# Bias groups one to a step, a third bias buffer and larger zero transfers in a fused attention and mixture-of-experts kernel

## The chip, the cores and the metric

The kernel runs on one core of one Trainium2 chip. The metric is the device time of one execution in microseconds (us), lower is better; a time is the median of several executions. Engines are named as in the profile: PE is TensorE (matmuls; PEld its weight loads), DVE is VectorE, ACT is ScalarE, POOL is GpSimd, SP is the sync engine, which here issues nearly all DMA transfers from one queue, in program order. TensorE's granted clock is given as a share of 2.4 GHz.

## What is computed

Attention with a learned relative bias over B = 2, H = 8 heads, S = 576 positions and D = 64, then a routed layer of eight experts (top 1, capacity 288), then a dense layer with a cosine gate. The change lies in the attention and in the setting up of the routed layer's buffers.

```python
def _attn_ref(q, k, v, w1, b1, w2):
    scores = scale * np.matmul(q, k.transpose(0, 1, 3, 2))
    ...
    x = (psi_rel / psi_i)[..., None]            # of the two positions alone
    h = np.maximum(x @ w1 + b1, 0.0)            # 32 hidden values per pair
    bias = h @ w2                               # one value per head
    scores = scores + bias.transpose(2, 0, 1)[None, :, :, :]
    scores = scores - np.max(scores, axis=-1, keepdims=True)
    attn = np.exp(scores)
    attn = attn / (np.sum(attn, axis=-1, keepdims=True) + 1e-09)
    return np.matmul(attn, v)
def _moe_ref(x, w_gate, w1, w2, capacity):      # tokens go to disp[e, pos] of their expert,
    ...                                         # rows beyond its count stay empty
def _moe2_ref(x, w_in, w_out):
    h = x @ w_in
    return (h * np.cos(h)) @ w_out
```

The bias depends on the positions alone, so it is made once for the five blocks of rows and used for both batches.

## The kernel before

Query rows are cut into five blocks ib, four of 128 rows and one of 64 (ib 4). They are worked on in the order 0, 1, 4, 2, 3, each for batch 0 and then 1; only block 4 takes both batches at once and is called the joint block. That makes nine blocks of four head pairs, 36 steps n; steps 0 to 7 are block 0, 8 to 15 block 1, 16 to 19 the joint block, 20 to 27 block 2, 28 to 35 block 3. The queues' order is that of the program: one loop (L775) writes for each n the scores of step n + 1 (`emit_qk`, L343, two heads, with the sum of scores and bias on VectorE at L363, which also gives the row's extreme), the transposes of step n (L386, evicted by ScalarE at L393), the exponential of step n + 1 (L372), and the product with v of step n - 1 (L402, L405).

Between them the bias is made, in 36 groups: 8 for each block of 128 rows, 4 for the joint block. A group has four h tiles of 128x576 (`bias_h`, L288 on VectorE or L286 on ScalarE), two halves of four matmuls (`bias_half`, L311) into one PSUM buffer psb that ScalarE evicts (L312) into one of three ev buffers, and a transfer (`bias_out`, L297 or L301) that spreads the rows over the bias buffer of its block. Groups 0 to 7 come before the loop in a form of their own (`bias_whole`, L318, and L326), groups 8 and 9 just ahead of it. The table `RUNS` (L53) says which groups a step makes: groups 10 to 19 in steps 0 to 9, none in 10 to 13, two in each of 14 to 17, one in each of 18 to 25. It has to be so because there are two bias buffers, bias_a and keep, used in turn by the blocks in their order, and a buffer takes a new block only when the old one is read.

Split precision: q and k are kept as a high part (a cast, `load_q` L272, `load_k` L241) and a low part, the subtraction at L273 and L245. GpSimd does the low part of k and, after the first block, that of q; VectorE does the first ones. `load_step` (L731) brings k and v along in the early steps; raw k passes through three buffers.

The routed layer needs rows of disp that no token fills to hold zeros and an invalid index, and the output to be zero where no row arrives. From step 5 to 13 `fill_rows` (L742) sends them on SP's queue: each disp part of 144 rows as a transfer of 128 rows and one of 16, and for every other part 128 rows of zeros to the output. Routing work (`late`, run one piece a step) begins at step 14 (`ROUTE_FROM`); its products lp (L484) and its sums (L551) read a free quarter of a transposes' PSUM tile, and its scatters (L572) run on GpSimd after the fills.

Of the kernel before, what the change touches and what calls it, by code (L numbers as in the profile page):

```python
# [21 lines left out]
NP = H // 2  # L22
# [30 lines left out]
RUNS = {n: (g,) for g, n in [(10 + i, i) for i in range(10)] + [(28 + i, 18 + i) for i in range(8)]}  # L53
RUNS.update({14 + i: (20 + 2 * i, 21 + 2 * i) for i in range(4)})
# [53 lines left out]
def attention_moe_kernel(  # L108
# [100 lines left out]
    kr_p = rpool("kr_p", 1)  # L209
# [52 lines left out]
    def load_q(b, ib, lo_eng, on_act=False):  # L262
        raw = raw_t.pop(("q", b, ib))
# [9 lines left out]
        lo_eng.tensor_tensor(out=c, in0=raw, in1=a.bitcast(F32), op=ALU.subtract)  # L273
# [44 lines left out]
    def bias_whole(g):  # L318
        ev_t[g] = keep[:, g, :]
# [23 lines left out]
    def emit_qk(n, u):  # L343
# [8 lines left out]
        for half in range(2):  # L352
# [42 lines left out]
    def emit_pv(n):  # L395
# [1064 lines left out]
```

## Time and profile before

| | us |
|---|---|
| median of 3 executions | 450.65 |
| lowest, highest | 450.21, 454.18 |
| profiled execution, its own time | 454.37 |
| its span, first to last instruction | 452.6 |
| PE, DVE, ACT, POOL busy | 405.5, 333.0, 287.2, 89.1 |
| mean granted clock of TensorE | 0.972 |

The span is one execution as the hardware profiler saw it. Busy times are sums over stages with different limits, so the stretches of time are to be read one by one. "Idle before" with an arrow names what ended an engine's wait. The attention's steps take the first 230 us, the experts and the dense layer the rest.

### The profile page before, as it was taken

To read this page: it belongs to the slowest core of one execution; us is meant where nothing else is said; L and a number is where in the kernel's file an instruction comes from. 1 tells how busy PE (TensorE), PEld (TensorE's weight loads), DVE (VectorE), ACT (ScalarE), POOL (GpSimd) and SP (SyncE) were. 2 spreads that over 40 slices of the span, in tenths; PEclk is the share of its full clock that TensorE was granted. 3 is DMA by queue.
4 is the path that set the end of the run, shared out by engine and by line. 5 is a ranking of instruction groups with operands and counts; after the bars stand their busy time and mean duration, and the time that the engine had idled before them with its cause. 6 is when DMAs were issued, how large, how long until landed. Compare 5 with 4: busy or idle time off the path is not lost. (4 is left out here: it accounts for less than half of the span.)

```text
span 452.6 us, 9167 instructions
## 1 busy us (share of the span) xinstructions
PE 405.5 (90%) x3326; PEld 321.4 (71%) x3326; DVE 333.0 (74%) x809; ACT 287.2 (63%) x651; POOL 89.1 (20%) x129
## 2 busy tenths in 40 slices
PE   8958798998978999999988959988899999999992
PEld 6435565786434677697768949976588998999981
DVE  3789999768566578679864996978956787787750
ACT  5747767876355678887863735545666766666561
POOL 1005523200022122223062343000730000000004
PEclk9989999999799999999998999998999999999997
DMA  6696565788923323282449009999320222210003
GB/s 212 170 319 182 163 172 182 197 234 255 281 89 109 85 54 100 65 252 95 141 131 354 1 16 348 308 300 386 103 90 0 95 55 86 93 49 0 1 1 114
DMA packets 48495, 66.64 MB, mean 147 GB/s; under 512 B 7125, under 2 KB 30037, under 8 KB 48442
## 3 DMA queue, kind: packets, MB, share of 16 engines
q1 hardware_dynamic: 47273, 63.50, 46.8%
q0 software_dynamic: 1168, 2.48, 1.5%
q8 instruction: 28, 0.46, 0.4%
q14 instruction: 26, 0.20, 0.2%
HBM read 43.97 MB, written 11.54 MB: 123 GB/s over the span
## 5 line engine op out<-in xcount | busy, mean ns | idle before, releaser
L288 DVE TENSOR_SCALAR h<-tt,sml 128x576 f32<-128x576 f32 x124 | 72.0, 630 | 9.7 <-PE psb L311 9.7
L372 ACT ACTIVATE e<-e,mn 128x576 f32<-128x576 f32 x72 | 55.9, 776 | 16.0 <-DVE mn L363 16.0
L311 PE MATMUL psb<-h,sml 128*32 128x288 f32 x448 | 40.6, 431 | 10.5 <-ACT wo L312 10.2
L362 PE MATMUL pss<-k,qh 128*128 128x288 f32 x128 | 42.4, 347 | 3.7 <-DVE k L245 3.7
L405 PE MATMUL xb<-et,wi 128*64 128x128 f32 (+1 forms) x640 | 41.4, 272 | 0.0
L362 PEld LDWEIGHTS pss<-k,qh 128*128 128x128 f32 x128 | 24.4, 191 | 22.9 <-issue 18.8
L1277 PE MATMUL z<-yh,s1h 128*128 128x384 f32 (+1 forms) x128 | 39.7, 310 | 0.9 <-DVE yl L1230 0.9
L1277 PE MATMUL z<-yh,s1l 128*128 128x384 f32 (+1 forms) x128 | 39.5, 309 | 0.0
L1277 PE MATMUL z<-yl,s1h 128*128 128x384 f32 (+1 forms) x128 | 39.5, 309 | 0.0
L312 ACT ACTIVATE wo<-psb,sml 128x288 f32<-128x288 f32 x56 | 28.0, 500 | 16.9 <-PE psb L311 16.8
L363 DVE CUSTOM_DVE_ANT_0 e<-pss,keep 128x576 f32<-128x576 f32 x32 | 24.1, 755 | 19.8 <-PE pss L362 19.8
L363 DVE CUSTOM_DVE_ANT_0 e<-pss,bias 128x576 f32<-128x576 f32 x40 | 30.0, 750 | 9.2 <-PE pss L356 6.4
L362 PE MATMUL pss<-k,ql 128*128 128x288 f32 x128 | 36.3, 298 | 0.0
L405 PEld LDWEIGHTS xb<-et,wi 128*64 128x64 f32 x640 | 32.4, 139 | 4.5 <-issue 0.2
L1302 PE MATMUL oacc<-s2h,gh 128*128 128x512 f32 x80 | 31.2, 390 | 0.4 <-ACT gh L1327 0.4
L1302 PE MATMUL oacc<-s2h,gl 128*128 128x512 f32 x80 | 31.3, 391 | 0.0
L1302 PE MATMUL oacc<-s2l,gh 128*128 128x512 f32 x80 | 31.2, 390 | 0.0
L1317 DVE TENSOR_TENSOR tn<-tn,kn 128x640 f32<-128x640 f32 (+2 forms) x18 | 13.5, 752 | 21.6 <-ACT kn L1314 21.6
L970 PE MATMUL acc<-hl,s2h 128*128 128x288 f32 x64 | 20.9, 326 | 8.2 <-DVE hl L983 8.1
L273 POOL TENSOR_TENSOR ql<-qraw,qh 128x1024 fp32r<-128x1024 f32 x7 | 16.7, 2381 | 51.1 <-DVE qh L272 39.6
L1290 POOL DMA_INDIRECT out_dram<-o,id x5 | 4.9, 983 | 109.6 <-ACT o L1289 108.3
L311 PEld LDWEIGHTS psb<-h,sml 128*32 128x32 f32 x448 | 9.1, 110 | 23.1 <-ACT wo L312 16.6
(713 smaller groups left out, 1113.6 us busy)
## 6 DMA issues: line engine op xcount, KB each, us to landing
keep<-win SPq DMA_DIRECT2D x16, 512.0 KB
keep<-wout SPq DMA_DIRECT2D x16, 512.0 KB
w1r<-mw SPq DMA_DIRECT2D x12, 512.0 KB
w2r<-mw SPq DMA_DIRECT2D x12, 512.0 KB
disp<-wo SPq DMA_DIRECT2D x18, 258.0 KB
keep<-wo SPq DMA_DIRECT2D x16, 288.0 KB
qraw<-qd SPq DMA_DIRECT2D x8, 512.0 KB
wi<-kd SPq DMA_DIRECT2D x6, 576.0 KB
```

Source lines behind the costliest of these rows:

```text
L273: lo_eng.tensor_tensor(out=c, in0=raw, in1=a.bitcast(F32), op=ALU.subtract)
L288: V.tensor_scalar(out=h, in0=win_, scalar1=col, scalar2=0.0, op0=ALU.add, op1=ALU.max)
L311: T.matmul(out=ps[32 * j:32 * j + 32, :], lhsT=w2s, rhs=h_t[g, j][:, c0:c0 + 288], start=True, stop=True)
L312: A.activation(out=ev_t[g][:, c0:c0 + 288], in_=ps, func=AF.Copy, scale=rst[:, g:g + 1])
L362: T.matmul(out=ps[:, half, 0:288], lhsT=w[b, ib][:, h, :], rhs=kp[b, p][:, u, cols], start=(i == 0), stop=(i == 1))
L363: V.tensor_tensor_reduce(out=e_t[n][:, u].rearrange("p (a c) -> p a c", a=2), in0=ps[:, :, 0:288], in1=bias_t[ib][:, h].rearrange("p (a c) ...
L372: A.activation(out=e_t[n][:, u], in_=e_t[n][:, u], func=AF.Exp, scale=-1.0, bias=mn_t[n][:, u:u + 1], accum_out=z_t[b, ib][:, h:h + 1],)
L405: T.matmul(out=xo[64 * u:64 * u + 64], lhsT=v[:, 64 * (4 * u + j):64 * (4 * u + j) + 64], rhs=et[:, 5 * u + j, a:e], start=False, stop=(j ...
L970: T.matmul(out=acc[d], lhsT=a[g % 3][:, 128 * d:128 * d + 128], rhs=x[m % 2], start=(m == 0 and i == 0), stop=(m == 7 and i == 2),)
L1277: T.matmul(out=sums(f, i), lhsT=w[f % 3][:, k], rhs=x[:, k, o0 + a:o0 + e], start=(k == 0 and n == 0), stop=(k == 3 and n == 2),)
L1302: T.matmul(out=acc_[t], lhsT=x, rhs=b[f % 3], start=(f == 0 and n == 0), stop=(f == 15 and n == 2))
L1317: V.tensor_tensor(out=tn, in0=tn, in1=kn, op=ALU.subtract)
```

## The change

Bias: `RUNS` now gives one group to each of steps 0 to 26, groups 9 to 35. A third bias buffer takes the joint block; it is made of the part of the weight buffer wi through which raw k passed in the early steps. Block 0 uses keep, block 1 bias_a, block 2 keep, block 3 bias_a. A joint group is written to partitions 0 to 63 alone, and behind the last one transfer copies these to 64 to 127. In steps 6, 18 and 26 (`SOON`), whose group is the last of a block that the next step begins to read, the two halves stand at the front of the step. One group (8) is left ahead of the loop; the first step's sums come behind its halves.

q, k, v: the low part of q is VectorE's from now on, in two halves in the last two steps of the block before. The first k and q are brought in among the groups 0 to 7. Raw k has four buffers. The tiles of v are cut up to fit beside them, and two small buffers are added.

Fills: disp in ten transfers of 256 rows and one of 32 in steps 7 to 12; the output's nine in steps 15 to 23. The order in which columns of wi are filled later (`PIECE`) follows the new layout.

```diff
-RUNS = {n: (g,) for g, n in [(10 + i, i) for i in range(10)] + [(28 + i, 18 + i) for i in range(8)]}
-RUNS.update({14 + i: (20 + 2 * i, 21 + 2 * i) for i in range(4)})
+RUNS = {n: n + 9 for n in range(27)}
+SOON = 6, 18, 26
...
-    kraw = [wi[:, 2 * i:2 * i + 2, 1280:1280 + S] for i in range(2)]
+    KC = 1024 - S
+    kraw = [wi[:, i].rearrange("p (u s) -> p u s", u=2)[:, :, KC:1024] for i in range(4)]
...
-    bias_t = {ib: (bias_a, keep)[i % 2] for i, ib in enumerate(IBS)}
+    bias_t = {0: keep, 1: bias_a, 4: wi, 2: keep, 3: bias_a}
+    joint = wi.rearrange("p k (x s) -> p (k x) s", x=2)[:, :, KC:1024]
...
-        lo_eng.tensor_tensor(out=c, in0=raw, in1=a.bitcast(F32), op=ALU.subtract)
+    def load_q_lo(b, ib, hs=slice(0, H)):
+        if b != BOTH:
+            V.tensor_tensor(out=ql[b, ib][:, hs], in0=raw_t["q", b, ib][:, hs], in1=qh[b, ib][:, hs].bitcast(F32), op=ALU.subtract)
...
-            for c in range(B):
-                for rr in range(2):
-                    Y.dma_start(out=bt[64 * c + r + rr:64 * c + 64:8], in_=ev[64 * rr:64 * rr + 64])
+            for rr in range(2):
+                Y.dma_start(out=joint[r + rr:64:8], in_=ev[64 * rr:64 * rr + 64])
+            if r == 6:
+                Y.dma_start(out=joint[64:128], in_=joint[0:64])
...
+    among = {
+        1: (lambda: fetch_k(0, 2),),
+        3: (lambda: load_k(0, 0, on_act=True),),
+        4: (lambda: load_k_lo(0, 0, V),),
+        5: (lambda: load_q(*first_q, on_act=True),),
+        6: (lambda: load_q_lo(*first_q),),
+    }
     for g in range(8):
...
         bias_whole(g)
         bias_whole_out(g)
-    load_k(0, 0, on_act=True)
-    load_q(0, IBS[0], V, on_act=True)
-    warm(28)
-    load_k_lo(0, 0, V)
+        for f in among.get(g, ()):
+            f()
...
-    def fill_rows(k):
-        for j in range(k, k + 2):
-            Y.dma_start(out=disp[144 * j:144 * j + 128, :], in_=zr)
-            Y.dma_start(out=disp[144 * j + 128:144 * j + 144, :], in_=zr[0:16])
-            if j % 2 == 0:
-                Y.dma_start(out=out[64 * j:64 * j + 128, :], in_=zr[:, :DM])
+    LOADS = {-1: 2, 0: 3, 1: -1, 2: 4, 3: 5, 4: 6, 5: 7}
...
+    def fill_rows(a, n=256):
+        k = -(-n // 128)
+        Y.dma_start(out=disp[a:a + n, :].rearrange("(p k) d -> p k d", k=k), in_=zr[0:n // k, None, :].to_broadcast([n // k, k, RW]))
...
-                elif p == 2:
-                    load_q(*BLOCKS[j + 1], P)
+                if p == 2:
+                    load_q(*nb)
+                if p > 1:
+                    load_q_lo(*nb, slice(4 * p - 8, 4 * p - 4))
...
+            if soon:
+                bias_half(g, 0)
             emit_qk(n + 1, 0)
         if n < ns:
             emit_tr(n, 0)
+            if soon:
+                bias_half(g, 1)
...
-        if 5 <= n < 14:
-            fill_rows(2 * (n - 5))
+        if 7 <= n < 12:
+            for i in range(2):
+                fill_rows(256 * (2 * (n - 7) + i))
+        if n == 12:
+            fill_rows(2560, E1 * CAP - 2560)
+            fill_ids()
+        if 15 <= n < 24:
+            fill_out(n - 15)
```

`LOADS` says which k a step casts (the number is its place in the order of use); -1 stands for the second block's q.

The order shows three places. VectorE on the way from the last groups ahead of the loop to the first sums, before (k_346 and ql are the first k and q, k_382 the second k; L363 is the first sum):

```order
L288 TENSOR_SCALAR h<-tt,sml 128x576 x3
L329 TENSOR_SCALAR keep<-pss,sml 128x288 x2
L273 TENSOR_TENSOR ql<-qraw,qh 128x1024
L245 TENSOR_TENSOR k_346<-wi,k_346 64x1152
L685 TENSOR_SCALAR tt<-tt,sml 128x448
L241 CAST k_382<-wi 128x1152
L363 ISA e,mn<-pss,bias_130 128x576
```

And now (k_272 is the first k, k_401 the second, L397 the sum):

```order
L266 TENSOR_TENSOR k_272<-wi,k_272 64x1152
L312 TENSOR_SCALAR h<-tt,sml 128x576 x2
L354 TENSOR_SCALAR bias_126<-pss,sml 128x288
L312 TENSOR_SCALAR h<-tt,sml 128x576 x3
L354 TENSOR_SCALAR bias_126<-pss,sml 128x288
L297 TENSOR_TENSOR ql<-qraw,qh 128x1024
L354 TENSOR_SCALAR bias_126<-pss,sml 128x288
L718 TENSOR_SCALAR tt<-tt,sml 128x448
L262 CAST k_401<-wi 128x1152
L312 TENSOR_SCALAR h<-tt,sml 128x576
L266 TENSOR_TENSOR k_401<-wi,k_401 64x1152
L397 ISA e,mn<-pss,keep 128x576
```

The two subtractions moved in among the groups; the subtraction of the second k and one h tile now stand ahead of the first sum.

GpSimd from its first work for the steps to the first routing, before:

```order
L245 TENSOR_TENSOR k_477<-kraw,k_477 64x1152
L245 TENSOR_TENSOR k_542<-wi,k_542 64x1152
L273 TENSOR_TENSOR ql<-qraw,qh 128x1024
L245 TENSOR_TENSOR k_616<-wi,k_616 64x1152
L245 TENSOR_TENSOR k_686<-kraw,k_686 64x1152
L245 TENSOR_TENSOR k_760<-wi,k_760 64x1152
L273 TENSOR_TENSOR ql<-qraw,qh 128x1024
L496 TENSOR_SCALAR nm<-top 128x1
```

And now:

```order
L266 TENSOR_TENSOR k_430<-wi,k_430 64x1152
L266 TENSOR_TENSOR k_495<-wi,k_495 64x1152
L266 TENSOR_TENSOR k_638<-wi,k_638 64x1152
L266 TENSOR_TENSOR k_710<-wi,k_710 64x1152
L266 TENSOR_TENSOR k_779<-wi,k_779 64x1152
L529 TENSOR_SCALAR nm<-top 128x1
```

The q subtractions left GpSimd's queue; the five of k stayed.

TensorE in step 14, from the second transposes to the scores of step 16, before (pst__1517 holds transposes, k_829 is the k of step 15, xb the product with v):

```order
L386 MATMUL pst__1517<-ident,e 128x128 x3
L432 MATMUL pst__1517<-ident,wo 128x128
L311 MATMUL psb<-h,sml 32x288 x4
L362 MATMUL pss<-k_829,qh 128x288
L362 MATMUL pss<-k_829,ql 128x288
...
L311 MATMUL psb<-h,sml 32x288 x4
L386 MATMUL pst__1544<-ident,e 128x128 x3
L311 MATMUL psb<-h,sml 32x288 x4
L402 MATMUL xb<-et,wi 128x128
L405 MATMUL xb<-et,wi 64x128 x8
L311 MATMUL psb<-h,sml 32x288 x4
L356 MATMUL pss<-k_346,qh 64x288
```

And now (k_860 is the k of step 15, v_127 its v):

```order
L420 MATMUL pst__1508<-ident,e 128x128 x3
L465 MATMUL pst__1508<-ident,wo 128x128
L336 MATMUL psb<-h,sml 32x288 x4
L389 MATMUL pss<-k_860,qh 128x288
L389 MATMUL pss<-k_860,ql 128x288
...
L420 MATMUL pst__1532<-ident,e 128x128 x3
L435 MATMUL xb<-et,v_127 128x128
L438 MATMUL xb<-et,v_127 64x128 x8
L336 MATMUL psb<-h,sml 32x288 x4
L383 MATMUL pss<-k_272,qh 64x288
```

Of the four sets of bias matmuls two are left in this step.

## Rows read from the trace of the kernel before

**Rows 1.** Busy time by stretch: us, then each engine's busy time, granted clock, DMA.
```profile
core 0: us, PE busy (x) PEld busy (x) DVE busy (x) ACT busy (x) POOL busy (x), PEclk, DMA share, GB/s
20.00:37.30 17.30, 11.56 (x120) 7.54 (x116) 14.32 (x22) 9.11 (x16) 2.79 (x1) 0.90 0.90 278
37.30:73.20 35.90, 31.13 (x302) 20.96 (x296) 35.72 (x63) 24.77 (x63) 15.79 (x6) 1.00 0.56 159
...
110.40:149.60 39.20, 32.91 (x319) 16.60 (x317) 22.36 (x67) 20.07 (x51) 7.33 (x16) 0.91 0.58 171
149.60:193.40 43.80, 43.80 (x494) 31.38 (x494) 31.45 (x95) 33.42 (x86) 8.22 (x15) 1.00 0.29 79
...
113.50:119.20 5.70, 5.70 (x38) 2.99 (x38) 1.81 (x4) 2.14 (x5) 0.00 (x0) 0.50 0.84 256
```
**Rows 2.** Waits from 110.4 to 149.6 us: who for whom, us in total, times, longest.
```profile
PE psb L311 <- ACT wo L312: 6.3, 7, 2.4
```
**Rows 3.** Timeline of DVE around 111 us: start, us, engine, line, operation, tiles.
```profile
108.75 1.78 DVE L288 TENSOR_SCALAR h<-tt,sml 128x576 f32<-128x576 f32 x4
110.44 0.75 DVE L363 CUSTOM_DVE_ANT_0 e<-pss,keep 128x576 f32<-128x576 f32 x1
...
111.11 0.22 DVE L484 TENSOR_TENSOR lp<-pst__1499,rz 128x64 f32<-128x64 f32 x1
```
**Rows 4.** Timeline of ACT and of PE there; in brackets the idle time and its releaser.
```profile
111.43 0.49 ACT L393 ACTIVATE et<-pst__1499 128x384 f32<-128x384 f32 x1 [2.78 <-DVE lp L484]
...
113.50 1.19 PE L311 MATMUL psb<-h,sml 128*32 128x288 f32 x8 [2.35 <-ACT wo L312]
```
**Rows 5.** Groups of PE instructions from 149.6 to 193.4 us: busy us, mean ns.
```profile
L311 PE MATMUL psb<-h,sml 128*32 128x288 f32 x128 | 11.1, 418 | 0.0
```
**Rows 6.** Timeline of DVE at the entry of the loop.
```profile
24.10 1.22 DVE L273 TENSOR_TENSOR ql<-qraw,qh 128x1024 fp32r<-128x1024 f32 x1 [1.48 <-ACT qh L270]
25.35 1.35 DVE L245 TENSOR_TENSOR k<-wi,k 64x1152 fp32r<-64x1152 f32 x1
...
33.14 4.20 DVE L288 TENSOR_SCALAR h<-tt,sml 128x576 f32<-128x576 f32 x4
37.26 0.74 DVE L363 CUSTOM_DVE_ANT_0 e<-pss,bias 128x576 f32<-128x576 f32 x1
```
**Rows 7.** Timeline of ACT there: the casts of the first k and q.
```profile
21.97 1.15 ACT L239 ACTIVATE k<-wi 128x1152 fp32r<-128x1152 f32 x1
23.02 1.04 ACT L270 ACTIVATE qh<-qraw 128x1024 fp32r<-128x1024 f32 x1
```
**Rows 8.** Timeline of DVE: pairs of h tiles.
```profile
29.24 0.95 DVE L288 TENSOR_SCALAR h<-tt,sml 128x576 f32<-128x576 f32 x2
...
41.99 4.70 DVE L288 TENSOR_SCALAR h<-tt,sml 128x576 f32<-128x576 f32 x2
...
68.52 2.74 DVE L288 TENSOR_SCALAR h<-tt,sml 128x576 f32<-128x576 f32 x2
```
**Rows 9.** Timeline of POOL from 40 to 72 us.
```profile
40.77 3.04 POOL L245 TENSOR_TENSOR k<-wi,k 64x1152 fp32r<-64x1152 f32 x1 [4.61 <-DVE k L241]
43.89 2.47 POOL L273 TENSOR_TENSOR ql<-qraw,qh 128x1024 fp32r<-128x1024 f32 x1
...
68.16 2.35 POOL L273 TENSOR_TENSOR ql<-qraw,qh 128x1024 fp32r<-128x1024 f32 x1 [5.49 <-DVE qh L272]
```
**Rows 10.** Timeline of DVE at 205 and 211 us: a shift of the weight narrowing.
```profile
205.27 2.16 DVE L669 TENSOR_SCALAR wi<-wi 128x512 int32<-128x512 int32 x1
...
211.42 0.41 DVE L669 TENSOR_SCALAR wi<-wi 128x512 int32<-128x512 int32 x1
```
**Rows 11.** Timeline of SP (group 35's transfer) and of DVE (its first reader).
```profile
193.20 0.54 SPq L297 DMA_DIRECT2D bias<-wo  x1
...
197.08 0.76 DVE L363 CUSTOM_DVE_ANT_0 e<-pss,bias 128x576 f32<-128x576 f32 x1 [1.13 <-PE pss L362]
```

More of the change, by code (lines that the diff above doesn't have):

```diff
@@ L169, in attention_moe_kernel @@
     cut = lambda a, n: flat[:, a:a + n]
-    rows = [cut(RW * t, RW) for t in range(10)]
-    xs_buf = [cut(10 * RW + NP * 128 * i, NP * 128).rearrange("p (q t) -> p q t", q=NP) for i in range(2)]
-    base = 10 * RW + 2 * NP * 128
+    rows = [cut(RW * t, RW) for t in range(9)]
+    xs_buf = [cut(9 * RW + NP * 128 * i, NP * 128).rearrange("p (q t) -> p q t", q=NP) for i in range(2)]
+    base = 9 * RW + 2 * NP * 128
     lt_buf = cut(base, 128)
@@ L221, in attention_moe_kernel, with v_of, bias_of @@
     w1s, b1s, w2s, rst, pst = (sml[:, a:c] for a, c in SMALL_AT)
-    kp, vt = {}, {}
-    kraw.append(kr_p.tile([128, 2, S], F32, name="kraw"))
+    kp = {}
     bias_a = bias_p.tile([128, H, S], F32, name="bias0")
-    bias_t = {ib: (bias_a, keep)[i % 2] for i, ib in enumerate(IBS)}
+    bias_t = {0: keep, 1: bias_a, 4: wi, 2: keep, 3: bias_a}
+    joint = wi.rearrange("p k (x s) -> p (k x) s", x=2)[:, :, KC:1024]
+    v12 = kv_p.tile([128, 2, 640], F32, name="v12")
+    v_parts = {
+        (i // 4, i % 4): [(0, KC, beside[x]), (KC, 640, beside[y][:, z:z + 640 - KC])]
+        for i, (x, y, z) in enumerate([(0, 1, 0), (2, 1, 192), (3, 4, 0), (5, 4, 192), (6, 7, 0)])
+    }
+    for p in (1, 2):
+        v_parts[1, p] = [(0, 640, v12[:, p - 1])]
+    v_parts[1, 3] = [(0, 640, v13)]
+    def v_of(b, p, a, n):
+        for lo, hi, t in v_parts[b, p]:
+            if lo <= a and a + n <= hi:
+                return t[:, a - lo:a - lo + n]
+    def bias_of(ib, h):
+        if bias_t[ib] is wi:
+            return joint[:, h]
+        return bias_t[ib][:, h]
     raw_t = {}
     def fetch_k(b, p):
-        raw = kraw[(NP * b + p) % 3]
+        raw = kraw[(NP * b + p) % 4]
         Y.dma_start(out=raw, in_=kd[b, :, 2 * p:2 * p + 2, :])
@@ L247, in load_v @@
     def load_v(b, ps):
-        vt[b] = vt_buf[b]
         for p in ps:
-            Y.dma_start(out=vt[b][:, p], in_=vp[b, :, p])
+            for lo, hi, t in v_parts[b, p]:
+                Y.dma_start(out=t, in_=vp[b, :, p, lo:hi])
     qh, ql = {}, {}
@@ L318, in bias_whole @@
     def bias_whole(g):
-        ev_t[g] = keep[:, g, :]
+        ev_t[g] = bias_a[:, g, :]
         ps = ps_s.tile([128, 2, 512], F32, tag="s", name="pss")
@@ L400, in emit_pv @@
             xo = xb[:, 128 * (n % 2) + a:128 * (n % 2) + e]
-            v = vt[c][:, p]
-            T.matmul(out=xo, lhsT=v[:, 512:640], rhs=et[:, 4, a:e], start=True, stop=False)
+            T.matmul(out=xo, lhsT=v_of(c, p, 512, 128), rhs=et[:, 4, a:e], start=True, stop=False)
             for j in range(4):
@@ L809, in attention_moe_kernel @@
             emit_tev(n, 1)
-        for g in nxt[:1] if len(gs) < 2 else ():
-            bias_h(g, on_act=ON_ACT if n < ACT_TO else (), quads=(0, 1))
+        if nxt is not None:
+            bias_h(nxt, on_act=ON_ACT if n < ACT_TO else (), quads=(0, 1))
         if n in EARLY:
```

112 lines of the change are left out of this document (60 added, 52 removed).

## The prediction

> **What bounds the kernel now.** I read the attention stretch by stretch, because the share of busy time over the whole span says little [rows 1]. A step's borders are the starts of its first score sum on VectorE (L363). Three kinds of stretch show. From 20 to 37.3 us no engine is full: this is the way from the first bias groups to the first sum of step 1. From 37.3 to 73.2 us (sums of steps 1 to 7) VectorE is busy 35.72 of 35.90 us and bounds. From 149.6 to 193.4 us TensorE is busy without a break, eight steps in 43.8 us, 5.5 us each with one bias group; there the matmuls of the steps themselves are the limit. Between them lies the odd one, 110.4 to 149.6 us: four steps take 39.2 us, 9.8 us each, TensorE sits idle for 39.20 - 32.91 = 6.29 us, and its granted clock is 0.50 of full speed (1.2 instead of 2.4 GHz) from 113.5 to 119.2 us.
>
> The waits of that stretch give nearly all the idle time one cause: TensorE's bias matmul waited for ScalarE's eviction of the single bias PSUM buffer, 6.3 us in 7 waits [rows 2]. Followed back at the longest of them: VectorE made the four h tiles of the second group (L288, 108.75, 1.78 us) before the sum at 110.44 and the logits product lp at 111.11 [rows 3]. ScalarE could not evict the transposes at 111.43 until lp had read the same PSUM tile, 2.78 us of idling, so its bias eviction came late too. TensorE stood still for 2.35 us until 113.50, and ran at half clock behind that [rows 4].
>
> **The change, part by part.** The sum is made against the profiled execution, 454.37 us (span 452.6 and 1.8 around it). That lies 3.7 us over the median of the three runs, 450.65, and I carry the difference in microseconds over to the median.
>
> *Groups spread evenly.* The groups 20 to 27 leave the four double steps and stand one to a step in 11 to 18; the order shows it for step 14, four matmul sets of the bias before, two now. TensorE's own work for them is the same, so in steps 10 to 17 only idle time and slow clock can go. Idle: 6.29 us. Clock: 5.70 us at half speed is 2.85 us of work lost. The most that can go is 9.1 us. Some of the routing waits stay (lp and the sums of the routing sit in VectorE's order as before), but four fewer h tiles stand ahead of them, and the eight full steps after 149.6 us, which also route, have no idle time. I leave 0.8 us of idling: -8.3 us. Bounds: if half the idling and the slow clock stay, -4; if all goes, -9.1.
>
> *One group moves from the entry into the loop.* The loop now makes groups 9 to 35. A group costs TensorE 11.1 / 8 = 1.39 us where TensorE bounds: 128 matmul records for eight groups [rows 5]. It falls on step 26, which had none: +1.4 us.
>
> *The entry.* Before, ScalarE's casts of the first k and q and VectorE's two subtractions stood behind all eight groups: 1.22 us for ql at 24.10, 1.35 us for k at 25.35. In front of these VectorE idled, 1.48 us before ql alone [rows 6]. Now they stand among the groups. The group loop grows by what they cost there, ScalarE 1.15 + 1.04 us [rows 7], VectorE 1.22 + 1.35 = 2.57 us, less the gaps that they fill; I take 2 us, so the last group's eviction ends at 24.6 instead of 22.6. From there VectorE's list is: 0.45 (tt), 0.67 (cast of k, start to start), one h 0.43, subtraction 1.36: 27.5. The sums need the last bias transfer; issued near 24.8, it lands at most 3.9 us later (below), 28.7. Two sums of 0.75, the accumulator reads and a cast of k: 30.9. Three h tiles, one held by GpSimd's subtraction as at 33.14, where four took 4.20 instead of the 1.78 of rows 3, so 2.4 + 1.4 us: 34.7. Before, sum 1 began at 37.26. That is -2.6; TensorE runs ahead of it. In it are four h tiles fewer on VectorE (group 10). Bounds: -4.5 if the casts vanish in the gaps, 0 if the loop grows by all of 2.6 us and the transfer queues behind the earlier fetch of k.
>
> *The q subtraction goes from GpSimd to VectorE* (one half per step). In the stretch that VectorE bounds, an h tile is stretched whenever GpSimd subtracts: two take 4.70 us at 41.99 and 2.74 at 68.52, where an undisturbed pair takes 0.95 [rows 8], and these are the moments of GpSimd's operations on k and q, 2.35 to 3.04 us each [rows 9]. Of the six in this stretch the four on k stay. The two on q go. At 41.99 the k one still ran for 40.77 + 3.04 - 41.99 = 1.8 us, so the q one held h for 4.70 - 0.95 - 1.8 = 2.0 us, and the second for 2.74 - 0.95 = 1.8 us. VectorE now does both itself, 1.22 us each by the one that it did at 24.10. 2 x 1.22 - 3.8 = -1.4 us. Bounds: +0.8 (a gap of TensorE's takes the place) to -3.8. In the TensorE-bound stretch VectorE has 43.8 - 31.5 = 12.3 us to spare, and the halves cost nothing but some of that; if a half of 0.6 us delayed each sum behind it, the ten remaining halves would cost 6 us, but sums there begin after 0.5 to 1.9 us of waiting for TensorE. I take 0. At 205 us a narrowing step takes 2.16 instead of 0.41 us beside the last q operation [rows 10], 1.75 us lost; now 1.22 us, -0.5.
>
> The Trainium skill's page "SBUF — State Buffer" (section "Who interferes with whom") says that a VectorE instruction with two SBUF inputs also excludes a GpSimd one that reads SBUF, whoever comes first blocking the other entirely. Rows 8 and 9 show that only for the one-input h. By this rule of the Trainium skill the moved subtractions could be held up like the h tiles.
>
> *The last group of a block comes later.* Groups 15, 27 and 35 are made in the step just before their first reader (steps 6, 18, 26), at its front. A set of four bias matmuls, the scores, three transposes, a second set and an eviction (0.7 + 0.65 + 0.35 + 0.7 + 0.5) put the transfer's issue 2.9 us into the step; it lands within 3.9 us: group 35's was issued at 193.20, and the sum that reads it started at 197.08, held by TensorE and not by it [rows 11]. So it is there at the latest 6.8 us in. The reader comes at 5.5 + 0.75 = 6.2 us in a plain step, later in step 18 (its scores are the joint block's, in fp32) and in step 6 (VectorE is behind TensorE there). +0.5 us, bounds 0 and +2.
>
> *Joint block in its own buffer, zeros.* The sum's in1 is another address, same size. The filling takes 11 transfers instead of 36 and starts two steps later; the output's nine zeros go behind. Scatters need it at the end of step 15; TensorE's steps hide it. 0; it costs if that cover is gone, see the slow rival. Also 0: 28 warming matmuls less, five more parts of v (both in the entry, where TensorE idles), the other order of the weight columns, one copy of 1.2 MB from partitions 0 to 63 to 64 to 127, read five steps later.
>
> Sum: -8.3 + 1.4 - 2.6 - 1.4 - 0.5 + 0.5 = **-10.9 us**; 454.4 - 10.9 = 443.5 for an execution like the profiled one, 450.65 - 10.9 = **439.8 us** for the median.
>
> **Rivals.**
> *VectorE gains nothing (b).* The moved subtractions meet GpSimd's k operations and are held for 2 us each: +2.6 instead of -1.4, 443.8 us. For it: every fast h tile that met one was held. Against: in the new order only the half of step 5 stands right behind a k operation, and there it would be held in place of the h tile that comes next; the whole one of step 1 has sums and h tiles in between. By the Trainium skill's page named above this would be the outcome if all of them overlapped.
>
> *The stall moves (c).* Routing begins at step 14 in either kernel; if lp and the routing sums hold ScalarE all the same, TensorE idles for 4 us and the slow clock stays: -2.3 instead of -8.3, and if the entry's gain drowns in DMA as well, 450.65 - 10.9 + 6.0 + 2.6 = 448.4 us, no measurable change. Against: the wait at 111.43 had four extra h tiles in front.
>
> *The late group stalls TensorE (d), slower.* If the transfers of groups 15, 27 and 35 land 2.5 us or more after their reader's turn, TensorE idles as long as at 111 us and the half clock follows, 2.85 us each time. The price is 3 x (2.5 + 2.85) = 16 us, 455.9 us. It decides from 6.2 + 2.35 = 8.5 us into the step on, so when other transfers hold the queue for 2 us or more: a q fetch of 512 KB is issued in each of these steps, and at the 278 GB/s of the entry [rows 1] it takes 1.9 us. Against: it starts ahead, while the matmuls still run. The Trainium skill's page "DMA: Bandwidth & Descriptors" (section "Queues, rings and completion order") has every SDMA engine take descriptors in ring order, which is for this rival; no row here shows it.
>
> *The change does less than it says (e).* The large fills and the wait before the 64-partition copy keep SP's queue so long that scatters, and GpSimd's small routing work behind them, come late: say 3 us at each of two routes, 445.8 us. Against: 2592 rows of 2064 B are 5.3 MB, 19 us at that rate from step 7 on, and the scatter comes eight steps, some 45 us, after it.
>
> **How the numbers follow.** Forecast 0.68, (b) 0.12, (c) 0.10, (d) 0.05, (e) 0.05. A measurement of this kernel tells about 1% (4.5 us) from no change: the runs lie within 4 us. The forecast, (b) and half of (e) are faster by more than that: 0.83. (c) and the rest of (e): 0.12. (d): 0.05. The bounds add up to a gain between 0.3 us (4 + 0 - 0.8 + 0.5 - 1.4 - 2) and 16.5 us (9.1 + 4.5 + 3.8 + 0.5 - 1.4). At the low end all of them would have to fail together, so I cut it at 3.7 us, which leaves out (c) and (d). Range 434 to 447 us.
>
> **What would show it.** Right: no double step, 10 to 17 at 5 to 6.5 us each and TensorE's clock 1.0 from step 10 to step 19; no wait of bias matmuls for the eviction over 1 us there; the first sum of step 1 by 35 us; no GpSimd operation over 2 us after step 4; step 26 longer by 1.4 us. Wrong: half clock after step 6, 18 or 26 with VectorE's sum waiting for a bias transfer (d); TensorE waiting for evictions in steps 14 to 17 as before (c); q subtractions of 2 us and more (b); GpSimd's first scatter held by the filling (e).

## The result, and the profile after

The changed kernel takes 454.67 us (median; 452.93 to 457.25), the kernel before 451.64 us beside it. The ratio is 1.0057, 95% interval 1.0035 to 1.0079: slower by 0.6%, clear of the noise, though no change by the prediction's own bound of 1%. The forecast was 439.8 us, range 434 to 447. The prediction was wrong.

Starts of the first score sum of a step, in us of each profiled execution, and the span. The last five columns are runs of the section below (e6 and e9 carry several edits).

| step | before | after | e1 | e2 | e4 | e6 | e9 |
|---|---|---|---|---|---|---|---|
| 1 | 37.3 | 33.4 | 32.3 | 32.3 | 31.9 | 32.0 | 33.5 |
| 7 | 73.2 | 77.7 | 71.5 | 71.1 | 75.9 | 67.1 | 67.4 |
| 11 | 93.5 | 98.4 | 92.5 | 91.8 | 96.8 | 90.9 | 88.1 |
| 19 | 149.6 | 149.8 | 143.9 | 143.0 | 144.0 | 138.1 | 134.0 |
| 26 | 187.8 | 187.8 | 181.8 | 180.9 | 181.9 | 176.0 | 172.4 |
| 31 | 209.8 | 212.1 | 206.1 | 205.1 | 206.3 | 200.3 | 194.4 |
| 35 | 227.1 | 229.3 | 223.3 | 222.3 | 223.6 | 217.5 | 211.6 |
| span | 452.6 | 454.0 | 452.2 | 448.6 | 449.5 | 442.0 | 433.9 |

Read the second and third column as differences. The entry gained 3.9 us. Steps 1 to 6 then lost 8.4 (35.9 before, 44.3 now). Steps 11 to 18, the place of the double steps, gained 4.6 (56.0 to 51.4) where 8.3 were forecast. Steps 26 to 30 lost 2.3. That makes +2.2 at step 35, and the rest of the kernel gives back 0.8 of it. These are the differences of two single executions: their spans lie 1.4 us apart, the medians 3.0. From step 35 to the end the executions of the table take between 222.3 us (e9) and 228.9 us (e1), though no experiment edits that part, so edits are compared by step starts as well as by the time.

Busy time by stretch in the changed kernel, cut at these starts, answers to [rows 1]:

```profile
core 0: us, PE busy (x) PEld busy (x) DVE busy (x) ACT busy (x) POOL busy (x), PEclk, DMA share, GB/s
20.00:33.40 13.40, 9.42 (x76) 4.84 (x74) 11.36 (x18) 6.78 (x13) 2.76 (x1) 1.00 0.86 257
33.40:43.55 10.15, 9.95 (x81) 6.64 (x80) 8.53 (x20) 8.31 (x20) 2.65 (x1) 0.83 1.01 286
43.55:77.70 34.15, 24.33 (x223) 16.21 (x222) 21.72 (x47) 18.09 (x44) 8.21 (x3) 0.90 0.37 100
77.70:119.23 41.53, 41.12 (x428) 29.50 (x427) 33.68 (x100) 32.20 (x85) 2.49 (x10) 1.00 0.62 166
119.23:149.83 30.60, 27.44 (x276) 15.56 (x275) 17.85 (x55) 16.89 (x44) 5.94 (x15) 0.94 0.64 189
149.83:194.47 44.64, 44.02 (x494) 31.37 (x495) 34.98 (x102) 33.37 (x86) 3.47 (x13) 1.00 0.41 118
194.47:212.07 17.60, 17.22 (x170) 14.20 (x168) 14.07 (x44) 14.65 (x40) 2.89 (x10) 1.00 0.74 215
```

Two rows stand out. From 43.55 to 77.70 us (steps 3 to 6) no engine is full any more. VectorE, which was busy without a break there before, works 21.72 of 34.15 us, and TensorE idles for 9.8 us, at a granted clock of 0.90. From 119.23 to 149.83 us TensorE idles for 3.2 us at a clock of 0.94. From 77.70 to 119.23, where groups 16 to 23 now stand one to a step, it is nearly full (41.12 of 41.53 us). The row from 43.55 also speaks against memory traffic as the reason there: a DMA share of 0.37.

The waits from 43.5 to 77.7 us (engine, line and what it waited for: us in all, times, longest) name the reason:

```profile
DVE e L397 <- PE pss L389: 12.1, 7, 3.6
PEld pss L389 <- POOL k L266: 10.1, 3, 4.0
PE pss L389 <- POOL k L266: 8.5, 3, 3.5
ACT wo L510 <- PE xb L508: 4.7, 1, 4.7
```

And the timeline (start, us, engine, line; in brackets the idle time and its releaser), GpSimd's three subtractions and the first of the scores that waited for them:

```profile
47.49 2.61 POOL L266 TENSOR_TENSOR k<-wi,k 64x1152 fp32r<-64x1152 f32 x1 [7.83 <-DVE k L262]
56.49 2.61 POOL L266 TENSOR_TENSOR k<-wi,k 64x1152 fp32r<-64x1152 f32 x1 [6.39 <-DVE k L262]
64.68 2.99 POOL L266 TENSOR_TENSOR k<-wi,k 64x1152 fp32r<-64x1152 f32 x1 [5.58 <-DVE k L262]
...
50.15 0.40 PE L389 MATMUL pss<-k,qh 128*128 128x288 f32 x1 [2.65 <-POOL k L266]
```

The scores of step 4 start at 50.15, when GpSimd's operation begun at 47.49 is done. Before, step n cast the key that step n + 3 needs. `LOADS` gives the slot of step 1 to the second q and casts keys 4 to 7 one step later: at the end of step n for scores at the front of step n + 1. Nothing is left between cast and reader but the subtraction itself. GpSimd waits for the cast, TensorE for GpSimd, VectorE's sums for TensorE, and the next cast stands behind these sums. In the kernel before TensorE nowhere waits for GpSimd in steps 1 to 6.

One wait of VectorE lies in the same stretch: the half of the q subtraction in step 5, against the next half, which met nothing.

```profile
65.24 2.98 DVE L297 TENSOR_TENSOR ql<-qraw,qh 128x512 fp32r<-128x512 f32 x1
...
76.85 0.69 DVE L297 TENSOR_TENSOR ql<-qraw,qh 128x512 fp32r<-128x512 f32 x1
```

It takes 2.98 us in place of 0.69 beside GpSimd's subtraction from 64.68 to 67.67. This is the one meeting that the prediction named under its rival (b), at about its price of 2 us.

The second place is at 121 us. SP's wait before the copy, and the timeline of SP (transfers as they are issued), ScalarE and TensorE:

```profile
SPq L326 <- DMA wi<-wo: 4.3, 1, 4.3
...
112.46 0.64 SPq L326 DMA_DIRECT2D wi<-wi  x1
113.14 3.21 SPq L793 DMA_DIRECT2D disp<-wo  x2
116.45 2.44 SPq L321 DMA_DIRECT2D keep<-wo  x1
118.93 3.36 SPq L793 DMA_DIRECT2D disp<-wo  x2
122.33 1.91 SPq L321 DMA_DIRECT2D keep<-wo  x1
...
107.94 0.50 ACT L337 ACTIVATE wo<-psb,sml 128x288 f32<-128x288 f32 x1 [0.19 <-PE psb L336]
...
124.98 0.50 ACT L337 ACTIVATE wo<-psb,sml 128x288 f32<-128x288 f32 x1 [3.12 <-DMA keep<-wo]
...
125.53 0.69 PE L336 MATMUL psb<-h,sml 128*32 128x288 f32 x8 [2.54 <-ACT wo L337]
```

L793 is a fill, 516 KB each; L326 the copy of the joint block, which can go only when the rows that it copies have landed; L321 the transfer of group 20 (116.45) and of group 21 (122.33). A bias row is evicted into one of three buffers, and group 23's eviction needs the one that group 20's transfer reads. Group 20's own eviction was over at 108.4. SP came to its transfer only at 116.45, behind the wait before the copy (4.3 us), the copy and two fills, and it was read out at 124.98, 8.5 us after its issue began; the eviction waited 3.12 us and TensorE 2.54. The kernel before has no bias group in steps 10 to 13, so no eviction there waits behind its fills.

The third is the reader of the last group, beside [rows 11]: SP's issue of group 35's transfer and VectorE's sum.

```profile
193.62 0.58 SPq L280 DMA_DIRECT2D qraw<-qd  x1
196.04 0.54 SPq L321 DMA_DIRECT2D bias<-wo  x1
...
200.08 0.76 DVE L397 CUSTOM_DVE_ANT_0 e<-pss,bias 128x576 f32<-128x576 f32 x1 [2.13 <-DMA bias<-wo]
```

The sum now waits 2.13 us for the transfer, where in [rows 11] it waited for TensorE alone.

### The profile page after: what moved, and what is told of

It is laid out like the page before. It is cut to its first block, busy times and chain, and to the rows that moved or that the text cites. A ratio compares the mean times of both kernels' runs of the same rounds, so it can differ in the third digit from the quotient of the medians.

```text
span 454.0 us, 9053 instructions
## 1 busy us (share of the span) xinstructions
PE 403.2 (89%) x3298; PEld 318.5 (70%) x3298; DVE 331.1 (73%) x822; ACT 288.8 (64%) x651; POOL 73.6 (16%) x122
## 4 chain that ended last, share of the span: by engine, by line
PE 31%; issue 31%; DMA 14%; DVE 11%; ACT 5%; POOL 4%; SPq 2%; ACTq 0%; POOLq 0%; DVEq 0%
PE pss L389 6%; PE psb L336 6%; PE xb L438 5%; POOL k L266 3%; DMA keep<-win 3%; DMA keep<-wout 2%; PE pss L383 2%; DMA w2r<-mw 2%; DVE e L397 2%; DMA keep<-wo 2%; DMA idl<-disp 2%; PE pss L348 2%; PE xb L435 1%; SPq L159 1%; DMA wi<-vp 1%
## 5 line engine op out<-in xcount | busy, mean ns | idle before, releaser
L312 DVE TENSOR_SCALAR h<-tt,sml 128x576 f32<-128x576 f32 x124 | 61.1, 535 | 0.1
L389 PE MATMUL pss<-k,qh 128*128 128x288 f32 x128 | 43.4, 354 | 10.2 <-POOL k L266 8.5
L336 PE MATMUL psb<-h,sml 128*32 128x288 f32 x448 | 42.2, 436 | 7.5 <-ACT wo L337 5.6
L389 PEld LDWEIGHTS pss<-k,qh 128*128 128x128 f32 x128 | 25.0, 195 | 33.4 <-issue 14.3
L397 DVE CUSTOM_DVE_ANT_0 e<-pss,keep 128x576 f32<-128x576 f32 x32 | 24.1, 755 | 24.2 <-PE pss L389 20.1
L397 DVE CUSTOM_DVE_ANT_0 e<-pss,bias 128x576 f32<-128x576 f32 x32 | 24.0, 751 | 9.8 <-PE pss L389 6.3
L1330 PEld LDWEIGHTS z<-yh,s1h 128*128 128x128 f32 x128 | 24.1, 188 | 1.9 <-DVE yl L1283 1.2
L438 PE MATMUL xb<-et,wi 128*64 128x128 f32 (+1 forms) x400 | 25.3, 269 | 0.0
L389 PEld LDWEIGHTS pss<-k,ql 128*128 128x128 f32 x128 | 24.9, 195 | 0.5 <-DVE ql L297 0.5
L1330 PEld LDWEIGHTS z<-yl,s1h 128*128 128x128 f32 x128 | 24.0, 188 | 0.5
L1330 PEld LDWEIGHTS z<-yh,s1l 128*128 128x128 f32 x128 | 24.1, 188 | 0.0
```

Source lines behind the costliest of these rows:

```text
L312: V.tensor_scalar(out=h, in0=win_, scalar1=col, scalar2=0.0, op0=ALU.add, op1=ALU.max)
L336: T.matmul(out=ps[32 * j:32 * j + 32, :], lhsT=w2s, rhs=h_t[g, j][:, c0:c0 + 288], start=True, stop=True)
L397: V.tensor_tensor_reduce(out=e_t[n][:, u].rearrange("p (a c) -> p a c", a=2), in0=ps[:, :, 0:288], in1=bias_of(ib, h).rearrange("p (a c) - ...
L438: T.matmul(out=xo[64 * u:64 * u + 64], lhsT=v_of(c, p, 64 * (4 * u + j), 64), rhs=et[:, 5 * u + j, a:e], start=False, stop=(j == 3),)
L1330: T.matmul(out=sums(f, i), lhsT=w[f % 3][:, k], rhs=x[:, k, o0 + a:o0 + e], start=(k == 0 and n == 0), stop=(k == 3 and n == 2),)
```

## The experiments

Theory A: the keys' casts come too late for the hand-over to GpSimd. Theory B: the joint block's copy holds SP's queue and so the bias transfers. Rivals: memory traffic (A2), and the large fills themselves (B2). All but e8 start from the changed kernel; ratios are to the kernel before, run on the same chip.

**e1: keys 4 to 7 one step earlier.**

```diff
-    LOADS = {-1: 2, 0: 3, 1: -1, 2: 4, 3: 5, 4: 6, 5: 7}
+    LOADS = {-1: (2,), 0: (3,), 1: (4, -1), 2: (5,), 3: (6,), 4: (7,)}
```

> Theory A: the casts of the second batch's four keys come one step too late, because the second query tile takes the slot of step 1; GpSimd's subtraction (about 3 us) then ends after TensorE wants the key. With keys 4 to 7 cast one step earlier each, steps 3 to 6 fall from 34.2 us (changed kernel) to 24.5 to 27, and the time from 454.7 to 443 to 447. Rival A2 (the slow steps come from the bus: value tiles and fills in the same stretch, or from the query tile's subtraction on VectorE): steps 3 to 6 stay above 31 us and the time within 2 us of 454.7.

450.77 us, ratio 0.992 (0.989 to 0.995). Steps 3 to 6 take 25.2 us, as theory A has it, and the waits for GpSimd's key are gone. The time gains less than the 8 to 12 us expected: by the two ratios 1.3%, 6 us, under the changed kernel. Step 2, for one, grew to 9.4 us. Timeline of VectorE and of GpSimd there:

```profile
41.52 0.73 DVE L262 CAST k<-wi 128x1152 fp32r<-128x1152 f32 x1
42.17 0.69 DVE L293 CAST qh<-qraw 128x1024 fp32r<-128x1024 f32 x1
42.89 3.54 DVE L297 TENSOR_TENSOR ql<-qraw,qh 128x1024 fp32r<-128x1024 f32 x1
...
42.33 3.02 POOL L266 TENSOR_TENSOR k<-wi,k 64x1152 fp32r<-64x1152 f32 x1 [2.88 <-DVE k L262]
```

The q subtraction, 1.22 us alone [rows 6], takes 3.54 us beside GpSimd's: it ends 1.1 us after GpSimd's end at 45.35. That is rival (b) of the prediction again, here with the whole second q. The Trainium skill's page "SBUF — State Buffer" (section "Who interferes with whom") says that a VectorE instruction with two SBUF inputs contends with a GpSimd one that reads SBUF, and that the one issued later is blocked; these two rows agree.

**e2: the low parts of all late keys on VectorE, casts where the changed kernel has them.**

```diff
-        load_k_lo(*ks[i], P if i + 1 < len(ks) else V)
+        load_k_lo(*ks[i], P if i < 4 else V)
```

> The same late casts, but the low parts of keys 4 to 7 all on VectorE, which needs no hand-over to GpSimd. Theory A in its narrow form (GpSimd's 3 us is what TensorE waits for): steps 3 to 6 fall by about 2 us each, to 26 to 29 us in all, time 447 to 450. If the late cast on VectorE itself is the cause (the cast stands behind the step's sums): only 0 to 1 us each, time 451 to 455. Rival A2: no change in steps 3 to 6.

449.28 us, ratio 0.990 (0.986 to 0.993). Steps 3 to 6 take 28.8 us. Waits from 42.34 to 71.09 us, and one of the subtractions:

```profile
PEld pss L389 <- DVE k L266: 8.0, 4, 2.3
PE pss L389 <- DVE k L266: 5.9, 4, 1.8
...
54.25 1.36 DVE L266 TENSOR_TENSOR k<-wi,k 64x1152 fp32r<-64x1152 f32 x1
```

1.36 us in place of 2.61, and the waits shrink, but TensorE still waits for the key in each of the four steps. So both are in it: the missing lead, and the length of GpSimd's operation.

**e14: e9 (below) with the low parts of keys 4 to 6 on GpSimd again, cast early.**

> The same kernel with the low parts of keys 4 to 6 back on GpSimd, still cast a step early. If the lead alone was missing (theory A in its first form): 435.5 to 437, no change. If two engines subtracting side by side hold each other (3.55 us for the query subtraction beside 3.02 us for the key's in the run with keys early): 2 to 5 us more, 438 to 441.

437.84 us, ratio 0.969 (0.961 to 0.976), where e9 has 0.965; step 35 begins 1.4 us later than in e9. With the lead, TensorE doesn't wait for GpSimd here either. Most of the loss was the lead; the engine is worth 1 to 2 us, and the whole second q subtraction takes 3.56 us again beside GpSimd's. The intervals overlap, so the time alone doesn't show that share.

**e4: one fill a step, steps 3 to 12.**

```diff
-        if 7 <= n < 12:
-            for i in range(2):
-                fill_rows(256 * (2 * (n - 7) + i))
+        if 3 <= n < 13:
+            fill_rows(256 * (n - 3))
```

> One large fill a step in steps 3 to 12 in place of two a step in steps 7 to 11; copy as in the changed kernel. Rival B2: the long issues (1.6 to 3 us each, at 102 to 126 us) go, the eviction's wait at 122 us goes, steps 11 to 19 fall by 2 to 3.5 us, time 451 to 453. Theory B: the wait of 4.3 us for the copy stays and the eviction still waits 1.5 to 3 us; time 453 to 455. If the fills now hold the keys' and values' transfers of steps 3 to 6, those steps grow over 34.2 us.

452.84 us, ratio 0.999 (0.995 to 1.003), some 0.7% under the changed kernel's ratio. Busy time in steps 15 to 18:

```profile
117.57:144.01 26.44, 25.82 (x276) 14.91 (x275) 17.80 (x55) 16.65 (x44) 6.08 (x15) 1.00 0.59 170
```

26.44 us where the changed kernel takes 30.60, clock 1.00, and the eviction's wait is gone, though SP still waits 4.4 us before the copy and single issues still take up to 2.6 us. SP comes to group 20's transfer at 109.44 in place of 116.45. From step 11 to 19 it is 47.2 us against 56.0 before: 8.8 us gained. Steps 3 to 6 stay at 33.9 us with a DMA share of 0.56 in place of 0.37: more traffic, and no slower.

**e3: the joint block's copy issued at the end of step 13** (L326 moved there).

> Theory B: the copy of the joint block's bias waits 4.3 us at the head of SP's queue in step 11, holds the fills and the next bias transfer behind it, and the eviction of step 14 finds its buffer still being read (3.1 us). With the copy issued at the end of step 13: the 3.1 us wait of the eviction at 122 us goes, steps 11 to 19 fall from 51.4 by 2 to 3.5 us, time 451 to 453. Rival B2 (the large fills fill the queue by themselves): the wait stays at over 2 us and the time within 1 us of 454.7.

462.18 us, ratio 1.018 (1.012 to 1.023): slower, and neither theory's time. The copy as SP issues it, the wait of VectorE's sum for it, and the q transfer issued right behind it (KB, us to landing); then the copy and the q transfers in e4:

```profile
120.23 0.62 SPq L907 DMA_DIRECT2D wi<-wi  x1
...
DVE e L395 <- DMA wi<-wi: 5.8, 1, 5.8
...
qraw<-qd SPq DMA_DIRECT2D x1, 512.0 KB, 12.3
...
wi<-wi SPq DMA_DIRECT2D x1, 1152.0 KB, 8.2
...
qraw<-qd SPq DMA_DIRECT2D x2, 512.0 KB, 5.3
```

The eviction's wait did go, with two fills a step as before: SP isn't held, and comes to group 20's transfer at 109.43. So the wait before the copy was needed for it, as theory B has it, and rival B2 in the form put here falls. But the copy, issued 7.8 us later, now lands just before 129.8 us, 9.6 us after its issue, and the sum of step 16 waits for it: steps 11 to 19 take 53.9 us in place of 51.4. Most of this flight is the copy's own: it takes 8.2 us in e4, where the last fill ahead of it was issued 10 us earlier. What else makes e3 slower isn't traced. The Trainium skill's page "DMA: Bandwidth & Descriptors" (section "Queues, rings and completion order") has each engine consume descriptors in ring order; the q transfer issued 0.7 us behind the copy takes 12.3 us to land, where it takes 5.3 in e4, which agrees.

**e12: the copy undone, four small transfers a group to both halves, as before.**

```diff
-            for rr in range(2):
-                Y.dma_start(out=joint[r + rr:64:8], in_=ev[64 * rr:64 * rr + 64])
-            if r == 6:
-                Y.dma_start(out=joint[64:128], in_=joint[0:64])
+            for c in range(B):
+                for rr in range(2):
+                    Y.dma_start(out=joint[64 * c + r + rr:64 * c + 64:8], in_=ev[64 * rr:64 * rr + 64])
```

> The changed kernel with one part undone: the joint block's bias is written to both halves by four small transfers a group, as before, and no copy. If the wait for the copy at the head of SP's queue made the eviction of step 14 late: the 3.1 us wait goes, steps 14 to 16 fall from 21.5 to 17 to 19 us, time 450 to 452.5. Rival (the large fills two a step do it alone, as the run with one fill a step suggests): within 1 us of 454.7, the wait at 122 us stays over 2 us.

459.45 us, ratio 1.014 (1.008 to 1.020): slower again. SP, the wait of the joint block's q cast, and that of the evictions:

```profile
107.10 2.08 SPq L280 DMA_DIRECT2D qraw<-qd  x2
109.28 8.80 SPq L325 DMA_DIRECT2D wi<-wo  x4
...
DVE qh L287 <- DMA qraw<-qd: 6.4, 1, 6.4
...
ACT wo L336 <- DMA wi<-wo: 4.4, 2, 2.3
```

Two fills a step and now four small transfers a group stand in the queue. Four issues take 8.80 us, the first of them alone 6.83. SP issues q at 107.10 instead of 100.99, and it comes 6.4 us late. Evictions still wait, 2.25 us at 113.97 and 2.10 at 124.72, now for the joint block's transfers. So theory B alone falls as well. In the changed kernel the wait of the eviction took both the wait before the copy and two fills a step: e3 takes away the one, e4 the other, and either ends it. But with two fills a step something else behind them is late each time, the copy in e3 and q in e12; of the three edits only thinner fills gain. That the rate of the fills is what matters in e12 is borne out by e11 and e9 below, with the same four transfers and one fill a step: there q is late by 1.4 and 0.4 us.

**e6: e1, e2 and e4 together.**

> The three edits together: keys 4 to 7 cast a step earlier, their low parts on VectorE, one large fill a step in steps 3 to 12. If the two causes (late keys, fills two at a time) are independent, the gains add: about 7 us from steps 2 to 6 and 5 to 6 us from steps 14 to 16, time 441 to 445 beside 454.7 of the changed kernel. If the first only moves a wait that the second also removes, 446 to 449. Both causes together account for the miss if the time comes to 443 or below.

443.32 us, ratio 0.981 (0.978 to 0.985). By the two ratios it lies 2.4% or 11 us under the changed kernel. By the same reckoning e1 gains 6, e2 7 and e4 3 us; e1 and e2 treat the same wait, so the gains of the two causes add as expected. Both account for the miss but for the last few microseconds: 443 or below was to be all of it.

**e5: each bias group one step earlier**, alone.

```diff
-RUNS = {n: n + 9 for n in range(27)}
-SOON = 6, 18, 26
+RUNS = {n: n + 10 for n in range(26)}
+SOON = ()
...
-    load_step(-1)
     bias_h(9, on_act=ON_ACT)
+    bias_half(9, 0)
+    bias_half(9, 1)
+    load_step(-1)
+    bias_h(10, on_act=ON_ACT)
```

> The changed kernel with each bias group one step earlier (two groups ahead of the loop, none in step 26). If the late last group costs what the trace of the changed kernel shows (VectorE waits 2.1 us for the landing at 200.1 us, step 26 takes 6.7 us in place of 5.6), steps 26 to 30 fall from 24.3 to 20.5 to 22 us and the entry grows by 1.4 to 2.6 us: time 452 to 455. Rival: the early group costs the entry as much as it gives back, and the stalls of steps 3 to 6 and 14 to 16 grow with it: 455 to 459.

455.58 us, ratio 1.011 (1.005 to 1.016), as the rival has it. Steps 26 to 30 fell from 24.3 to 22.4 us, and the way from the first sum to that of step 1 grew from 5.7 to 7.0; what was gained went into step 13, 10.7 us long, where the joint block's q came 6.2 us late.

**e7: e6 and e5 together.**

> As the run with three edits, and each bias group one step earlier as well. If the last group's landing wait is worth more than the entry's extra group: 1 to 2.5 us under that run. Rival: the entry pays it back, within 1 us of that run.

442.22 us, ratio 0.979 (0.974 to 0.984), not told apart from e6 by the interval. The q wait of e5 is there; SP ahead of it, and VectorE:

```profile
92.66 0.64 SPq L326 DMA_DIRECT2D wi<-wi  x1
93.36 0.62 SPq L793 DMA_DIRECT2D disp<-wo  x1
94.07 5.12 SPq L280 DMA_DIRECT2D qraw<-qd  x2
...
107.22 0.69 DVE L287 COPY qh<-qraw 128x1024 f32<-128x1024 f32 x1 [4.85 <-DMA qraw<-qd]
```

Here the 1152 KB copy and one fill stand right ahead of q.

**e9: e7 and e12 together.**

> As the run with all parts (keys early and on VectorE, one fill a step, groups one step earlier), and the joint block's bias written to both halves by four small transfers a group, as the kernel before does, in place of the 1152 KB copy. If the copy's wait on SP's queue and its size are what still holds step 13 (9.41 us there, with a query tile landing 11 us after its issue), step 13 falls to 5 to 6 us and the time to 437 to 440. Rival (the fills alone fill the queue): step 13 stays over 8 us and the time within 1 us of that run.

436.00 us, ratio 0.965 (0.962 to 0.968): faster than both kernels. Step 13 takes 5.0 us. Busy time by stretch:

```profile
46.20:67.44 21.24, 18.79 (x199) 13.21 (x198) 20.94 (x49) 16.03 (x42) 0.00 (x0) 1.00 0.69 196
67.44:108.87 41.43, 41.43 (x435) 29.59 (x434) 33.76 (x101) 33.04 (x87) 2.48 (x10) 1.00 0.78 216
108.87:134.00 25.13, 25.13 (x268) 14.75 (x267) 17.80 (x55) 16.17 (x43) 6.18 (x15) 1.00 0.38 112
```

VectorE is full again in steps 3 to 6 (20.94 of 21.24 us) and TensorE in steps 7 to 18, at clock 1.00. It lies 6 us under e7, where 2 to 5 were expected.

**e10: e7 with the copy in step 12 and the fills in steps 2 to 11.**

> As the run with all parts, with the copy kept but issued in step 12, when the fills, now in steps 2 to 11, are over. If the copy hurts only by its wait at the head of SP's queue: step 13 falls to 5 to 6 us, time 437 to 440. If it hurts by its size: the query tile or the bias transfers behind it are late in steps 13 to 15 instead, time 441 to 445.

439.50 us, ratio 0.973 (0.970 to 0.976). Its profiled execution, the fastest of its four, has the same steps as e9 (step 13: 5.0 us) and nearly the same span, 434.2 against 433.9 us: there the copy, 9.6 us in flight, delays no step, so in e7 it hurt by what it stood in front of. The fills are a step earlier too, and why its median is 3.5 us over e9's stays open.

**e11: e9 with the groups where the changed kernel has them.**

> As the run with three edits (443.3 us), and the joint block's bias written by four small transfers a group. There the copy cost no long step, so 0 to 2 us less: 441 to 444; the bias groups stay where the changed kernel has them.

443.61 us, ratio 0.981 (0.978 to 0.984). Against e6 the copy's removal is worth nothing there. Against e9, on the same chip, the earlier groups are worth 7.6 us.

**e8: the kernel before with the q subtraction on VectorE** (the engine at L273 changed for all tiles).

> The kernel before, with the query tiles' subtraction moved from GpSimd to VectorE and nothing else. The step of the prediction on this (1.4 us gained) gives 449 to 451 where the kernel before has 451.6; the stall of step 29 to 30 (5.24 us step) falls to 4.1. Rival: VectorE, now with 2 to 3 us more in one step of each block, delays the sums: 452 to 455.

455.40 us, ratio 1.007 (1.002 to 1.011). Its stretches for steps 1 to 6, 16 to 18 and 26 to 30:

```profile
37.27:74.42 37.15, 31.73 (x296) 22.00 (x291) 33.16 (x65) 25.70 (x63) 10.95 (x4) 0.92 0.57 160
122.70:154.48 31.78, 26.59 (x254) 13.17 (x253) 17.63 (x49) 14.85 (x37) 4.10 (x10) 0.89 0.40 113
193.42:214.29 20.87, 20.87 (x210) 17.48 (x210) 15.59 (x50) 17.89 (x48) 2.88 (x10) 1.00 0.63 184
```

Before they take 35.94, 27.68 and 22.02 us. The last gains 1.15 us, about what was expected. The first loses 1.2, with the whole q subtraction at 3.56 us beside GpSimd's, but it ran at a clock of 0.92, and the middle one at 0.89, where the kernel before had 1.00 in both. So neither these two nor the whole time price the edit.

**e13: e9 with the q subtraction on GpSimd again.**

> The kernel of the run with direct joint writes and all parts (436.0 us, ratio 0.965 to the kernel before), with the query tiles' subtraction put back on GpSimd (all but the first tile's). The prediction's step (VectorE's h tiles held 2 us by each GpSimd subtraction, 1.4 us lost in all, 0.5 at the narrowing): 437.5 to 440. Rival (VectorE pays as much for the subtraction as it is held): 435 to 437. If GpSimd's slower subtraction also makes TensorE wait for the second query tile: 440 or above.

437.21 us, ratio 0.968 (0.961 to 0.975). Step 35 begins 0.5 us later than in e9. The intervals overlap: the move is worth about half a microsecond, or nothing.

## Why the prediction was wrong

In the table "changed" is the difference to the kernel before by the step starts above, "mended" that of e9 (in the double steps also e4, which keeps the groups where the change has them).

| term | forecast | changed | mended |
|---|---|---|---|
| entry, to step 1 | -2.6 | -3.9 | -3.8 |
| steps 1 to 6 (q subtraction) | -1.4 | +8.4 | -2.0 |
| steps 11 to 18 (double steps) | -8.3 | -4.6 | -10.1 (e4: -8.8) |
| steps 26 to 30 (a group more, last group, narrowing) | +1.4 | +2.3 | -0.1 |

*The step that failed* is in the part on the q subtraction: "Of the six in this stretch the four on k stay." They stay on GpSimd, but the slot of the second q pushes the last keys' casts one step back, and the prediction has no term for that. The prediction counted how long GpSimd's operations are and what they hold up, and not how long before its reader each one starts. One step of lead is what hid 3 us of subtraction. e1 shows it: steps 1 to 6 fall from 44.3 to 39.3 us without a change of engine or of what is moved. Of the 3.3 us that e1 still takes over the kernel before, 2.1 stand in step 2, where q meets k, and 1.2 in step 6, with the late group. e2 shows the other side of the same wait.

*The second step that failed* is the zero for "Joint block in its own buffer, zeros", for the fills ("TensorE's steps hide it") and for the copy. The cover was looked for at the fills' own reader, the scatter, eight steps later, and there it holds. But the evenly spread groups put bias transfers into steps 10 to 13, where the kernel before has none, behind the wait before the copy and fills issued up to step 12; and each must be read out before the eviction three steps on. The runs show 3.12 us of waiting at that eviction, and 4.2 us more in steps 15 to 18 than in e4. Rival (e) had the mechanism, fills and a copy that hold the queue, with the wrong victim. The two parts of the change were priced singly, and the loss is in their meeting: e4 undoes it.

*The double steps* were right in mechanism and size. With one fill a step the stretch gains 8.8 us; 8.3 were forecast. The stall at 111 us did not move (rival c). e9 gains 10.1, over the 9.1 that the prediction called the most: 1.3 of it is step 18, 7.2 us in place of 8.4.

*The entry* was right in kind and too small: the sum of step 1 starts at 33.4 us, the forecast had 34.7. The first sum was forecast at 28.7 and starts at 27.7, where it did before. The gain lies behind it: three h tiles of 3.74 us (3.8 in the forecast) in place of eight of 6.1 us and a subtraction of k of 1.36. The same code in e1 to e4, e6 and e12 begins step 1 at 31.9 to 32.3 us, a gain of about 5 us, past the bound of 4.5.

*The q subtraction*, -1.4, was mis-sized: where e13 undoes it alone, steps 1 to 6 take 34.3 us against 33.9 in e9, 0.4 us. Rival (b) holds wherever a q subtraction meets one of k, as at 65.24 in the changed kernel and 42.89 in e1. The narrowing, -0.5, was right by the same pair: 22.5 against 22.0 us in steps 26 to 30.

*The group in step 26* was right: 6.7 us against 5.6 before, +1.2 for the 1.4 forecast.

*The last group of a block*, +0.5, was mis-sized. In the changed kernel the late keys hid step 6's share. With them mended, e11 against e9 shows steps 6 to 8 at 17.5 against 14.2 us, 18 to 20 at 20.1 against 19.1, and 26 to 30 at 24.3 against 22.0; 1.4 of the last is the group that e9 makes ahead of the loop. That is some 5 us at three places, against 0.6 more in the entry. Another 1.7 us between the two lie in steps 1 to 5; why is open. Rival (d) named the place; it came about without the drop to half clock (1.00 from 77.70 to 119.23 and from 149.83 to 212.07), and below its price.

e6 mends both failed steps, takes the keys' low parts from GpSimd besides, and keeps the late groups. It takes 443.3 us where the forecast's terms, which left those two steps at nothing, came to 439.8; the last group's cost over its 0.5 us is larger than that difference.

## What to carry to other kernels

For each producer that a change moves, write down how long before its reader it starts, in steps, and compare that with its duration plus the hand-over; a table of numbers that says "which tile in which step" is such an edit even where no instruction is added. A transfer's cover is to be sought at everything queued behind it, not at its own reader alone: bulk writes are thin enough when the small, urgent transfer behind them still lands within its own slack. And price parts that meet on one queue together.

## What was not expected of the hardware

An issue on SP, usually 0.5 to 0.7 us, can take far longer in the stretches with the fills: 2.44 us at 116.45 in the changed kernel, 4.75 at 99.25 in e7, 6.83 at 109.28 in e12. In each case the data were ready: the last eviction before it had ended at 108.4, 93.2 and 104.4 us. So not just landings are delayed there but the engine that issues. What exactly holds it isn't shown; e9 has one such issue too (5.02 us at 94.65) and loses no step by it. And taking the wait before the copy away from that queue (e3, e12) made the kernel about 1% slower, since the copy came late in the one, and q in the other.
